# Running the first four attention units of a fused kernel in chunks of 64 tokens, with one decay table instead of two

## The chip, the cores and the metric

The kernel runs on one core of one Trainium2 chip. The metric is device time in microseconds (us) of one execution. Five engines work beside each other, each through its own instructions in order: TensorE (PE; its weight loads are listed as PEld), VectorE (DVE), ScalarE (ACT), GpSimd (POOL) and SyncE (SP), which here only issues DMA transfers. An instruction that needs another engine's result, or a transfer's data, waits on a semaphore, and everything behind it on its engine waits too.

## The reference, cut to what matters

```python
def _attn_ref(q, k, v):                      # (4, 8, 576, 64) each
    scores = np.matmul(q, k.transpose(0, 1, 3, 2)) / np.sqrt(64)
    gamma = 1.0 - 2.0 ** (-5.0 - np.arange(8))
    rel = pos[:, None] - pos[None, :]
    Dmat = np.where(rel >= 0, gamma[:, None, None] ** rel, 0.0)
    return np.matmul(scores * Dmat, v)       # no softmax

x = attn_out.transpose(0, 2, 1, 3).reshape(2304, 512)
h = x @ w_in;  g = h * sigmoid(1.702 * h);  x = g @ w_out        # 512 -> 2048 -> 512
xn = x / sqrt(mean(x * x) + 1e-6) * rms_g
return (silu(xn @ w_gate) * (xn @ w_val)) @ w_out2               # 512 -> 1536 -> 512
```

The attention is linear: a decay per head and distance takes the place of the softmax. So it can be done in pieces of the sequence, with a state S (the decayed sum of k times v over all tokens before) carried from piece to piece. Within a piece the decay gamma^(i-j) is split into a factor for the query (gamma^i / 8, table `qdec`), one for the value (gamma^-j, table `vdec`) and a triangular mask; S is multiplied by a third table, `sdec`, from piece to piece.

## The kernel before

The 2304 tokens are cut into 18 *units* of 128 tokens. The first MLP then takes them in five blocks of 512, 384, 384, 512 and 512 tokens, the second in three of 768. All matmul operands of the MLPs are split in a high and a low part (each product is three matmuls, lines 283 to 285), so x of a unit has to be written as `xh` (rounded, by ACT) and `xl` (the rest, x minus xh).

Block 0 of the first MLP needs x of units 0 to 3, so those four run ahead of it: this is the *front*, written out by hand. The other fourteen units are threaded in between the matmuls of the MLP, in steps given by a table (`at_steps`).

A unit passes through these steps:

- load: q, k and v by DMA from the SP queue (q of unit 0 from ACT's), line 339; packets of 256 bytes
- `a_decay` (line 353): v is multiplied by `vdec` on POOL
- `a_trans` (line 364): eight PE transposes of k and q; ACT copies kT from PSUM (line 371)
- scores, mask, k times v, new state, and out, for which there are two forms

The *wide* form, only for units 0 to 3, takes all 128 tokens as one piece. qT is copied without a factor (lines 375 to 378). Scores are 8 matmuls with 128 columns (line 511), k times v another 8 (line 519), the mask is a multiply by a 128x128 triangle (line 525, DVE), out is 8 matmuls from v and the masked scores (line 569) and 8 from the state and qT (line 555). Only then does the decay of the queries come in, as a multiply on the output (`scaled`, line 583, DVE); ACT makes xh (line 586), POOL or DVE makes xl (line 589). Each unit has an x buffer of its own. Each step of the state is a sum and a multiply by `sdec` (lines 541 and 542).

The *chunk* form, for units 4 to 17, takes two pieces of 64 tokens. qT is multiplied by `qdec` as it leaves PSUM (line 373, DVE). Scores are 16 matmuls with 64 columns (line 396), k times v is 16 (line 405), the mask takes 64 columns per head (line 413), out is 16 matmuls plus 8 for each piece that has a state (line 475). ACT copies the two pieces from PSUM (line 484), DVE adds the two state parts (line 488), ACT makes xh (line 494), POOL xl (line 495). Here all units share one x buffer (`bufs=1`), so the copies of a unit wait until POOL has read x of the unit before.

The two forms want the query decay in different head layouts, so there are two tables in the one tile `qdec`: 256 KB for the front (line 1126, SP queue), and after the last `scaled` of the front a second one, spread over the partitions by two POOL transfers from a row in DRAM (`qrow`, lines 1092 and 1076).

Seven matmuls of a constant (`heat`, line 1103) run on PE before the first data is there. At the end of the front stand the first two weight tiles of the first MLP (`in_halves`: words on ACT, lines 203 and 206; join on DVE, line 209; high part on ACT, line 215; low part on DVE, line 218), and the third by `conv_words` and `conv_join` (lines 189, 190, 243, 252).

Of the kernel before, what the change touches and what calls it, by code (L numbers as in the profile page):

```python
# [21 lines left out]
XB = 512  # L22
# [20 lines left out]
def kernel(  # L43
# [47 lines left out]
    qrow = dram.tile([1, H * 128], F32, name="qrow")  # L91
# [265 lines left out]
    def a_trans(u, where):  # L357
        kr, qr = (raws[u, nm] for nm in "kq")
        pt = a_psum(where)

        more = ps_acc.tile([128, 512], F32, tag="acc", name="at") if u == 0 else pt[0]
        for i, t in ((1, kr), (0, qr)):
            for p in range(HP):
                nc.tensor.transpose(  # L364
                    (more if i == 0 and p > 1 else pt[i])[:, p * 128:(p + 1) * 128],
                    t[:, 2 * p:2 * p + 2, :].rearrange("p h d -> p (h d)"),
                    ident,
                )
        qT = a_tile(u, "qT")
        kT = a_tile(u, "kT")  # L370
        nc.scalar.copy(out=kT, in_=pt[1])
        if u > 3:
            nc.vector.tensor_tensor(out=qT, in0=pt[0], in1=qdec, op=ALU.mult)
        elif u == 0:
            nc.vector.tensor_copy(out=qT[:, :256], in_=pt[0][:, :256])
            nc.scalar.copy(out=qT[:, 256:], in_=more[:, 256:])
# [75 lines left out]
    def a_out(u, where):  # L452
# [30 lines left out]
        for c in range(2):  # L483
            nc.scalar.copy(out=xc[c], in_=po[c][:, :HP * C])
        for c in range(2):
            if old[c]:
                a, b = (t[:, 2 * C * (1 - c):][:, :2 * C] for t in (po[1 - c][:, HP * C:], xc[c]))
                nc.vector.tensor_tensor(out=b, in0=a, in1=b, op=ALU.add)
        x = x.rearrange("p (c a t) -> p a c t", c=2, t=C)
# [3 lines left out]
        def parts():  # L493
            nc.scalar.copy(out=xh, in_=x)  # L494
            nc.gpsimd.tensor_tensor(out=xl, in0=x, in1=xh.bitcast(F32), op=ALU.subtract)  # L495

        rows.append(parts)

    wide_mask = sp.tile([128, TH], F32, tag="norm", name="wide_mask", bufs=3)[:, :2 * C]

    def wide_scores(u, where, amid=lambda: None, own=None):
        qT, kT = st[u]
        sc = a_psum(where)
        for p in range(HP):
            for j in range(2):
                hs = slice(64 * j, 64 * j + 64)  # L510
                nc.tensor.matmul(  # L511
                    sc[j][:, p * 2 * C:(p + 1) * 2 * C], kT[hs, p, :], qT[hs, p, :], start=True, stop=True
                )
        amid()
        kr, vt = raws[u, "k"], raws[u, "v"]
        kv = (own or ps_h.tile([128, XB], F32, tag="h", name="kv"))[:, :HP * D]
        for p in range(HP):
            for j in range(2):
                nc.tensor.matmul(
                    kv[64 * j:64 * j + 64, p * D:(p + 1) * D], kr[:, 2 * p + j, :], vt[:, head(p, j), :],  # L520
                    start=True, stop=True,
                )
        r = [a_tile(u, f"r{j}").rearrange("p (a c) -> p a c", c=2 * C) for j in range(2)]
        for j in range(2):
            nc.vector.tensor_tensor(
                out=r[j], in0=sc[j].rearrange("p (a c) -> p a c", c=2 * C),
                in1=wide_mask.unsqueeze(1).to_broadcast([128, HP, 2 * C]), op=ALU.mult,
            )
        st[u] = (qT, r, kv.rearrange("p (a d) -> p a d", d=D))
        a_free(u, "kT", "k")  # L530

    def wide_state(u, ops=None):
        qT, r, kv = st[u]
        dec = sdec.unsqueeze(2).to_broadcast([128, HP, D])
        old = state["next"] if u else None
        state["next"] = new = att.tile([128, HP, D], F32, tag="S", name="S", bufs=4)
        st[u] = (qT, r, old)

        def sums():
            if old is not None:  # L540
                nc.vector.tensor_tensor(out=new, in0=kv, in1=old, op=ALU.add)
            nc.vector.tensor_tensor(out=new, in0=kv if old is None else new, in1=dec, op=ALU.mult)

        sums() if ops is None else ops.append(sums)

    def wide_at(po, h):
        j, half = h // HP, 64 * x_half(h)
        return po[j][half:half + 64, x_tile(h % HP) * 2 * C:][:, :2 * C]

    def wide_over(po, qT, old, first):  # L550

        for h in (0, 4, 1, 5, 2, 6, 3, 7):
            j, p = divmod(h, HP)
            hs = slice(64 * j, 64 * j + 64)
            nc.tensor.matmul(
                wide_at(po, h), old[hs, p, :], qT[hs, p, :], start=first and x_tile(p) == 0,
                stop=not first and x_tile(p) > 0,
            )

    def wide_out(u, where, po=None):  # L560


        qT, r, old = st.pop(u)
        vt = [raws.pop((u, nm)) for nm in "kqv"][2]
        begun = po is not None
        po = po or a_psum(where)
        for h in range(H):
            j, p = divmod(h, HP)
            nc.tensor.matmul(  # L569
                wide_at(po, h), vt[:, h, :], r[j][:, p, :], start=not begun and x_tile(p) == 0,  # L570
                stop=(begun or old is None) and x_tile(p) > 0,
            )
        if old is not None and not begun:
            wide_over(po, qT, old, False)
        n, o = block_of(2 * C * u)
        a_free(u, "v", "qT", "r0", "r1")
        xh, xl = (t[:, :, o:o + 2 * C] for t in block_tile(n))
        x = a_tile(u, "x")
        xs = x.rearrange("p (k t) -> p k t", t=2 * C)

        def scaled(j):
            js = slice(4 * C * j, 4 * C * j + 4 * C)
            nc.vector.tensor_tensor(out=x[:, js], in0=po[j][:, :4 * C], in1=qdec[:, js], op=ALU.mult)

        def high(ks=slice(0, 4)):
            nc.scalar.copy(out=xh[:, ks], in_=xs[:, ks])  # L586

        def low(ks=slice(0, 4), engine=nc.vector):
            engine.tensor_tensor(out=xl[:, ks], in0=xs[:, ks], in1=xh[:, ks].bitcast(F32), op=ALU.subtract)

        return scaled, high, low
# [422 lines left out]
    with tc.manual_schedule():  # L1014
# [6 lines left out]
        def a_both(u, where):  # L1021

            a_scores(u, where, True)
            a_out(u - 1, HID)
            a_state(u)
# [3 lines left out]
        phases.append((a_out, len(units) - 1))  # L1029
# [35 lines left out]

        a_load(0, "q", nc.scalar)
        a_load(0, "k")
        nc.gpsimd.dma_start(
# [4 lines left out]
        def spread_row(engine, t, row):  # L1073
# [6 lines left out]
        nc.gpsimd.memset(wide_mask, 1.0)  # L1080
        nc.gpsimd.affine_select(
            out=wide_mask, in_=wide_mask, pattern=[[1, 2 * C]], base=0, channel_multiplier=-1,
            compare_op=ALU.is_ge, fill=0.0,
        )
        nc.gpsimd.memset(mask, 1.0)
        for c in range(2):
# [5 lines left out]
        nc.gpsimd.dma_start(  # L1092
            out=qrow.rearrange("o (b e c) -> o b e c", e=2, c=128),
            in_=c_qdec[0:128:64].rearrange("e b c -> b e c").unsqueeze(0),
        )
# [30 lines left out]
        nc.sync.dma_start(out=qdec, in_=c_qdec.rearrange("q b c -> q (b c)"))  # L1126
# [8 lines left out]
        def load_begin(j):  # L1135
# [16 lines left out]

        a_trans(0, AT)
        wide_scores(0, ACC)
        wide_state(0)
        a_trans(1, AT)
        scaled, high, low = wide_out(0, ACC)
        wide_scores(1, ACC)
# [7 lines left out]
        scaled(0)  # L1166
        scaled(1)
        high()
# [8 lines left out]
        scaled, high, low = wide_out(2, ACC)  # L1177
        scaled(0)
        scaled(1)
        high()  # L1180
        join()
        wh()
        word1()
        po = a_psum(AT)
        wide_scores(
            3, ACC, lambda: wide_over(po, st[3][0], state["next"], True),
            ps_acc.tile([128, 512], F32, tag="acc", name="kv"),
        )
        low(engine=nc.gpsimd)
        held_back = []  # L1190
        wide_state(3, held_back)
        scaled, high, low = wide_out(3, ACC, po)
        to_conv.pop(0)
        scaled(0)
        high(slice(0, 2))
        wl()
        join1()
        low(slice(0, 2))
# [292 lines left out]
```

## Time and profile before

| what | before |
|---|---|
| time, median of 3 runs | 884.67 us (884.52 to 885.3) |
| the profiled execution's own time | 885.02 us |
| its span, first to last instruction | 883.3 us |
| PE busy | 876.1 us, 99% of the span |
| DVE, ACT, POOL busy | 512.8, 382.3, 92.0 us |
| first matmul of block 0 | at 24.52 us |
| last idle time of PE ahead of the tail | at 45.23 us, 0.5 us |

The profile is of one execution. Its times count from the first instruction. A timeline row gives start, duration, engine, line, operation, output tile and input tiles, partitions x elements, how many instructions were merged in the row, and in brackets how long the engine stood idle before it and what ended that. A duration of several merged instructions reaches from the first one's start to the last one's end; PE's matmuls overlap, so the distance between two starts tells the pace.

### The profile page before, as it was taken

To read this page: it belongs to the slowest core of one execution; us is meant where nothing else is said; L and a number is where in the kernel's file an instruction comes from. 1 tells how busy PE (TensorE), PEld (TensorE's weight loads), DVE (VectorE), ACT (ScalarE), POOL (GpSimd) and SP (SyncE) were. 2 spreads that over 40 slices of the span, in tenths; PEclk is the share of its full clock that TensorE was granted. 3 is DMA by queue.
4 is the path that set the end of the run, shared out by engine and by line. 5 is a ranking of instruction groups with operands and counts; after the bars stand their busy time and mean duration, and the time that the engine had idled before them with its cause. 6 is when DMAs were issued, how large, how long until landed. Compare 5 with 4: busy or idle time off the path is not lost.

```text
span 883.3 us, 16180 instructions
## 1 busy us (share of the span) xinstructions
PE 876.1 (99%) x6170; PEld 792.8 (90%) x6170; DVE 512.8 (58%) x918; ACT 382.3 (43%) x766; POOL 92.0 (10%) x100
## 2 busy tenths in 40 slices
PE   9999999999999999999999999999999999999998
PEld 7778889999999888888889999999999999999997
DVE  4778754464574555756645557765575666333444
ACT  3877754365445554564463343334322225112222
POOL 4201111131232212311200000000000000000000
PEclk9999999999999999999999999999999999999999
DMA  9986445689789987897777766557654556555552
GB/s 217 265 282 193 131 156 168 205 318 313 234 256 317 280 258 243 268 398 255 258 273 228 242 213 213 167 167 252 224 153 158 155 155 227 160 163 158 164 168 107
DMA packets 153200, 193.49 MB, mean 219 GB/s; under 512 B 66144, under 2 KB 94052, under 8 KB 153124
## 3 DMA queue, kind: packets, MB, share of 16 engines
q1 hardware_dynamic: 144212, 165.06, 60.0%
q10 hardware_dynamic: 8688, 27.14, 9.3%
q8 instruction: 49, 0.80, 0.4%
q0 software_dynamic: 224, 0.27, 0.1%
q14 instruction: 27, 0.22, 0.1%
HBM read 150.22 MB, written 42.21 MB: 218 GB/s over the span
## 4 chain that ended last, share of the span: by engine, by line
PE 96%; ACT 1%; DVE 1%; DMA 0%; issue 0%; SPq 0%; DVEq 0%; ACTq 0%
PE h L283 17%; PE h L285 17%; PE h L284 17%; PE acc L283 11%; PE acc L285 11%; PE acc L284 11%; PE v L284 2%; PE v L285 2%; PE v L283 2%; PE at L364 2%; PE at L475 1%; PE at L396 1%; PE at L405 1%; PE at L511 1%; DMA wslots<-in_k_dram 0%; PE at L569 0%
## 5 line engine op out<-in xcount | busy, mean ns | idle before, releaser
L283 PE MATMUL h<-fast 128*128 128x384 f32 (+1 forms) x824 | 288.4, 350 | 1.1 <-ACT fast L586 0.6
L285 PE MATMUL h<-fast 128*128 128x384 f32 (+1 forms) x824 | 287.1, 348 | 0.0
L284 PE MATMUL h<-fast 128*128 128x384 f32 (+1 forms) x824 | 286.6, 348 | 0.1
L917 DVE TENSOR_TENSOR wslots<-h,wslots 128x384 f32<-128x384 f32 x180 | 100.2, 556 | 151.6 <-PE h L285 151.2
L283 PE MATMUL acc<-fast 128*128 128x512 f32 (+1 forms) x464 | 174.9, 377 | 0.0
L285 PE MATMUL acc<-fast 128*128 128x512 f32 (+1 forms) x464 | 174.5, 376 | 0.0
L284 PE MATMUL acc<-fast 128*128 128x512 f32 (+1 forms) x464 | 174.3, 376 | 0.0
L283 PEld LDWEIGHTS h<-fast 128*128 128x128 f32 x824 | 154.7, 188 | 10.9 <-ACT fast L586 0.8
L284 PEld LDWEIGHTS h<-fast 128*128 128x128 f32 x824 | 154.8, 188 | 9.3 <-DVE fast L218 0.5
L285 PEld LDWEIGHTS h<-fast 128*128 128x128 f32 x824 | 154.6, 188 | 8.2 <-DVE fast L255 0.4
L609 DVE TENSOR_TENSOR fast<-g,fast 128x512 fp32r<-128x512 f32 (+1 forms) x80 | 53.9, 673 | 123.8 <-ACT fast L607 123.1
L950 ACT CAST fast<-g 128x384 fp32r<-128x384 f32 x36 | 18.5, 514 | 219.6 <-DVE g L920 219.6
L627 ACT ACTIVATE g<-h 128x512 f32<-128x512 f32 (+1 forms) x80 | 44.3, 553 | 136.4 <-PE h L285 136.4
L285 PEld LDWEIGHTS acc<-fast 128*128 128x128 f32 x464 | 87.1, 188 | 13.3
L283 PEld LDWEIGHTS acc<-fast 128*128 128x128 f32 x464 | 87.1, 188 | 12.7
L284 PEld LDWEIGHTS acc<-fast 128*128 128x128 f32 x464 | 87.1, 188 | 11.9
L868 DVE TENSOR_TENSOR wslots<-wslots 128x256 fp32r<-128x256 f32 x84 | 43.6, 555 | 14.8 <-ACT wslots L867 14.8
L840 POOL TENSOR_TENSOR wslots<-wslots 128x256 f32<-128x256 f32 x48 | 43.2, 919 | 76.0 <-DVE wslots L243 63.1
L607 ACT CAST fast<-g 128x512 fp32r<-128x512 f32 (+1 forms) x80 | 46.2, 578 | 2.5
L495 POOL TENSOR_TENSOR fast<-x,fast 128x512 fp32r<-128x512 f32 x14 | 18.7, 1339 | 227.5 <-ACT fast L494 203.8
L189 ACT ACTIVATE sslots<-sslots 128x512 f32<-128x512 f32 x56 | 37.7, 674 | 0.2 <-DMA sslots<-in_moe_w_out_dram 0.2
L190 ACT ACTIVATE sslots<-sslots 128x512 uint32<-128x512 uint8 x56 | 37.0, 661 | 0.0
(137 smaller groups left out, 872.2 us busy)
## 6 DMA issues: line engine op xcount, KB each, us to landing
fast<-up_d SPq DMA_DIRECT2D x252, 256.0 KB, 3.0
fast<-out_d ACTq DMA_DIRECT2D x51, 512.0 KB, 5.1
up_d<-wslots SPq DMA_DIRECT2D x84, 256.0 KB, 4.9
sslots<-in_moe_w_out_dram SPq DMA_DIRECT2D x19, 512.0 KB, 5.2
out_d<-fast SPq DMA_DIRECT2D x16, 512.0 KB, 3.6
sslots<-in_moe_w_in_dram SPq DMA_DIRECT2D x15, 512.0 KB, 4.9
sslots<-in_moe_w_val_dram SPq DMA_DIRECT2D x12, 512.0 KB, 6.4
sslots<-in_moe_w_gate_dram SPq DMA_DIRECT2D x11, 512.0 KB, 6.1
```

Of the source, the lines that this page charges most:

```text
L189: nc.scalar.activation(out=hi, in_=hi, func=AF.Prelu, scale=2.0 ** -112, alpha=-(2.0 ** 32))
L190: nc.scalar.activation(out=lo, in_=byte, func=AF.Copy, scale=1 / 32, bias=-31 / 64)
L283: nc.tensor.matmul(ps, lh, rh, start=first, stop=False, skip_group_check=more)
L284: nc.tensor.matmul(ps, *pairs[0], start=False, stop=False, skip_group_check=more)
L285: nc.tensor.matmul(ps, *pairs[1], start=False, stop=last, skip_group_check=more)
L495: nc.gpsimd.tensor_tensor(out=xl, in0=x, in1=xh.bitcast(F32), op=ALU.subtract)
L607: nc.scalar.copy(out=gh, in_=g)
L609: nc.vector.tensor_tensor(out=gl, in0=g, in1=gh.bitcast(F32), op=ALU.subtract)
L627: nc.scalar.activation(out=g, in_=ps, func=AF.Gelu_apprx_sigmoid)
L840: nc.gpsimd.tensor_tensor(out=o, in0=a, in1=b, op=op)
L868: nc.vector.tensor_tensor(out=wl.bitcast(F32R), in0=w, in1=wh, op=ALU.subtract)
L917: nc.vector.tensor_tensor(out=o, in0=a, in1=b, op=ALU.add)
```

## The change

Units 0 to 3 take the chunk form too. The whole wide form goes (`wide_scores`, `wide_state`, `wide_over`, `wide_out`, the 128x128 mask, the x buffer per unit). `a_out` hands back its four last steps (copies, adds, high, low), so that the front can order them by hand; `a_rows` keeps the old order for the later units.

The two tables give way to one in the layout of the chunk form. Columns 0 to 64 of it are loaded at the very start, in four transfers of 64 partitions x 2 x 65 numbers (`decay_load`: two from POOL ahead of everything there, two from SP behind k of unit 0); columns 65 to 127 are made by one DVE instruction as a product of two loaded ones.

```diff
+        nc.vector.tensor_tensor(out=qT, in0=pt[0], in1=qdec, op=ALU.mult)
         if u > 3:
-            nc.vector.tensor_tensor(out=qT, in0=pt[0], in1=qdec, op=ALU.mult)
-        elif u == 0:
...
-        else:
-            nc.scalar.copy(out=qT, in_=pt[0])
-        a_decay(u)
+            a_decay(u)
...
-        for c in range(2):
-            nc.scalar.copy(out=xc[c], in_=po[c][:, :HP * C])
...
+        def copies():
+            for c in range(2):
+                nc.scalar.copy(out=xc[c], in_=po[c][:, :HP * C])
...
+        return copies, adds, high, low
...
+        def decay_load(e, queue):
+            for j in range(2):
+                queue.dma_start(
+                    out=qdec[64 * j:64 * j + 64].rearrange("p (b e c) -> p b e c", b=2, e=2)[:, :, e, :C + 1],
+                    in_=c_qdec[64 * e:64 * e + 64, 2 * j:2 * j + 2, :C + 1],
+                )
+
+        decay_load(0, nc.gpsimd)
         a_load(0, "q", nc.scalar)
         a_load(0, "k")
+        decay_load(1, nc.sync)
...
-        nc.gpsimd.dma_start(
-            out=qrow.rearrange("o (b e c) -> o b e c", e=2, c=128),
...
-        nc.sync.dma_start(out=qdec, in_=c_qdec.rearrange("q b c -> q (b c)"))
...
+        q_c = qdec.rearrange("p (a c) -> p a c", c=2 * C)
+        nc.vector.scalar_tensor_tensor(
+            out=q_c[:, :, C + 1:], in0=q_c[:, :, 1:C], scalar=float(D) ** 0.5,
+            in1=q_c[:, :, C:C + 1].to_broadcast([128, HP, C - 1]), op0=ALU.mult, op1=ALU.mult,
+        )
+
+        def begin_scores(u):
+            a_scores(u, ACC, True)
+            a_state(u, (0,))
+
+        def begin_out(u):
+            copies, adds, high, low = a_out(u, HID)
+            copies()
+            adds()
+            high()
+            return low
...
-        low(engine=nc.gpsimd)
-        wide_state(1)
-        scaled, high, low = wide_out(1, ACC)
-        scaled(0)
-        scaled(1)
-        high()
-        wide_scores(2, ACC)
-        low(engine=nc.gpsimd)
-        wide_state(2)
+        a_state(1, (1,))
+        a_decay(2)
+        low = begin_out(1)
+        low()
+        begin_scores(2)
         a_trans(3, AT)
+        a_state(2, (1,))
+        a_decay(3)
         (word, join, wh, wl), (word1, join1, wh1, wl1) = in_halves(0)
         word()
...
+        low = begin_out(2)
+        low()
         join()
         wh()
+        begin_scores(3)
         word1()
...
+        copies, adds, high, low = a_out(3, HID)
+        copies()
+        join1()
+        adds()
+        wh1()
+        high(slice(0, 2))
+        wl()
+        low(slice(0, 2), nc.vector)
...
-        spread_row(nc.gpsimd, qdec, qrow)
```

How the instructions stand on the engines shows where work moved. First PE, from the scores of unit 3 to the first matmul of block 0. Before, in the wide form (line 511 scores, 555 state part of out, 519 k times v, 569 value part of out):

```order
L511 MATMUL at<-wslots 128x128 [waits Activation_49]
L511 MATMUL at<-wslots 128x128 [waits PE_49]
L511 MATMUL at<-wslots 128x128 x6
L555 MATMUL at<-wslots,S 64x128 [waits DVE_49,PE_49]
L555 MATMUL at<-wslots,S 64x128 [waits PE_49]
L555 MATMUL at<-wslots,S 64x128 x6
L519 MATMUL kv<-wslots 64x64 [waits DVE_49,Pool_49]
L519 MATMUL kv<-wslots 64x64 x7
L569 MATMUL at<-wslots 64x128 [waits DVE_49]
L569 MATMUL at<-wslots 64x128 x3
L569 MATMUL at<-wslots 64x128 [waits DVE_49]
L569 MATMUL at<-wslots 64x128 x3
```

The same place in the changed kernel (line 389 scores, 398 k times v, 468 out):

```order
L389 MATMUL at<-wslots 64x64 [waits DVE_49,Activation_49]
L389 MATMUL at<-wslots 64x64 x15
L398 MATMUL at<-wslots 64x64 [waits Pool_49]
L398 MATMUL at<-wslots 64x64 x15
L468 MATMUL at<-wslots 64x64 [waits DVE_49,Activation_49]
L468 MATMUL at<-wslots 64x64 x7
L468 MATMUL at<-wslots 64x64 [waits DVE_49]
L468 MATMUL at<-wslots 64x64 x7
L468 MATMUL at<-wslots,S 64x64 x8
L468 MATMUL at<-wslots,S 64x64 [waits DVE_49]
L468 MATMUL at<-wslots,S 64x64 x7
L282 MATMUL h<-fast 128x512 [waits Activation_49]
```

The state part of out, which stood ahead of k times v and of POOL's decayed v, now stands behind both, at the end of the unit.

Second ACT, from the first words of the weights to the last of x (before: line 586 makes xh; 203 and 206 words, 215 high part of weights):

```order
L203 ACTIVATE sslots<-sslots 128x256 [waits DMAHW5_49]
L206 ACTIVATE sslots<-sslots 128x256
L586 CAST fast<-wslots 128x4x128 [waits DVE_49]
L215 CAST fast<-ww 128x256 [waits DVE_49]
L203 ACTIVATE sslots<-sslots 128x256 [waits DMAHW7_49]
L206 ACTIVATE sslots<-sslots 128x256
L586 CAST fast<-wslots 128x2x128 [waits DVE_49,Activation_49]
```

In the changed kernel (line 482 copies x from PSUM, 491 makes xh; 202, 205 and 214 are the weights' lines):

```order
L202 ACTIVATE sslots<-sslots 128x256 [waits DMAHW6_49]
L205 ACTIVATE sslots<-sslots 128x256
L482 COPY x<-at 128x256 [waits PE_49,Pool_49]
L482 COPY x<-at 128x256 [waits PE_49]
L491 CAST fast<-x 128x4x128 [waits DVE_49,Activation_49]
L214 CAST fast<-ww 128x256 [waits DVE_49]
L202 ACTIVATE sslots<-sslots 128x256 [waits DMAHW0_49]
L205 ACTIVATE sslots<-sslots 128x256
L482 COPY x<-at 128x256 [waits PE_49,Pool_49]
L482 COPY x<-at 128x256 [waits PE_49]
L214 CAST fast<-ww 128x256 [waits DVE_49]
L491 CAST fast<-x 128x2x128 [waits DVE_49,Activation_49]
```

Two copies per unit came in on ACT, and the first of them waits for POOL, which reads the shared x buffer.

Third DVE, from the start to the first multiply of x of unit 0. Before:

```order
L375 COPY wslots<-at 128x256
L525 TENSOR_TENSOR wslots<-at,wide_mask 128x512 x2
L542 TENSOR_TENSOR S<-kv,sdec 128x256
L525 TENSOR_TENSOR wslots<-at,wide_mask 128x512 x2
L583 TENSOR_TENSOR wslots<-at,qdec 128x256 x2
```

In the changed kernel (line 1064 makes the rest of the table, 370 is qT, 406 the mask, 431 to 440 the state, 488 the adds):

```order
L1064 SCALAR_TENSOR_TENSOR qdec<-qdec 128x4x63
L370 TENSOR_TENSOR wslots<-at,qdec 128x512
L406 TENSOR_TENSOR wslots<-at,mask 128x4x64 x2
L431 COPY S<-at 128x256
L370 TENSOR_TENSOR wslots<-at,qdec 128x512
L439 TENSOR_TENSOR S<-at,S 128x256
L440 TENSOR_TENSOR S<-S,sdec 128x256
L488 TENSOR_TENSOR x<-at,x 128x128
```

The table `qdec`, first read by the multiply of the first output, is now read ahead of the first scores.

## Rows read from the trace of the kernel before

**Rows 1.** Busy time by stretch: start:end, length, engines' busy us, PEclk, DMA, GB/s.

```profile
8.60:24.50 15.90, 15.31 (x256) 12.64 (x252) 10.86 (x23) 7.19 (x16) 7.03 (x6) 1.00 1.14 262
```

**Rows 2.** PE's waits over the whole run: us in total, times, longest.

```profile
PE h L283 <- DVE fast L252: 0.5, 1, 0.5
```

**Rows 3.** Chain of waits from 24 to 46 us: start, us, what.

```profile
24.82 0.32 ACT sslots L206
...
27.04 0.74 ACT fast L215 x2
27.79 0.58 ACT sslots L189
...
28.96 0.70 DVE ww L243
29.69 0.62 ACT fast L252
...
44.66 0.44 DVE fast L252
...
45.23 0.47 PE h L283
```

**Rows 4.** Timeline, all engines, unit 3 at the end of the front.

```profile
18.48 0.42 PEld L364 LDWEIGHTS at<-ident,wslots 128*128 128x128 f32 x4 [0.24 <-PE at L364]
...
20.23 1.04 POOL L353 TENSOR_TENSOR wslots<-wslots,vdec 128x512 f32<-128x512 f32 x1 [1.12 <-DMA wslots<-in_v_dram]
...
22.36 1.28 POOL L589 TENSOR_TENSOR fast<-wslots,fast 128x512 fp32r<-128x512 f32 x1 [1.09 <-ACT fast L586]
...
24.07 0.40 ACT L586 CAST fast<-wslots 128x256 fp32r<-128x256 f32 x1 [0.84 <-DVE wslots L583]
...
24.52 0.50 PE L283 MATMUL h<-fast 128*128 128x512 f32 x1 [0.58 <-ACT fast L586]
```

**Rows 5.** Timeline, a later unit in chunk form; the first row is another unit's qT.

```profile
46.94 0.69 DVE L373 TENSOR_TENSOR wslots<-at,qdec 128x512 f32<-128x512 f32 x1
...
56.52 0.69 PE L396 MATMUL at<-wslots 64*64 64x64 f32 x32
57.03 0.65 PE L405 MATMUL at<-wslots 64*64 64x64 f32 x32
57.50 0.65 PE L475 MATMUL at<-wslots 64*64 64x64 f32 x32
57.80 0.76 DVE L413 TENSOR_TENSOR wslots<-at,mask 128x256 f32<-128x256 f32 x2 [1.92 <-PE at L405]
57.97 0.41 PE L475 MATMUL at<-wslots,S 64*64 64x64 f32 x16
...
58.43 0.65 ACT L484 COPY x<-at 128x256 f32<-128x256 f32 x2 [3.27 <-PE at L475]
...
59.11 0.29 DVE L488 TENSOR_TENSOR x<-at,x 128x128 f32<-128x128 f32 x1 [0.55 <-ACT x L484]
...
59.77 0.42 DVE L446 TENSOR_TENSOR S<-at,S 128x256 f32<-128x256 f32 x1
```

**Rows 6.** Timeline, all engines, units 0 and 1.

```profile
1.43 0.73 POOL L1068 DMA_DIRECT2D srow<-in_sdec_dram  x1 [0.92 <-POOLq L1473]
...
5.90 1.08 POOL L1076 DMA_DIRECT2D sdec<-srow  x2 [1.42 <-DMA srow<-in_sdec_dram]
...
7.23 1.94 PE L511 MATMUL at<-wslots 64*128 64x128 f32 x16 [0.18 <-DVE wslots L375]
...
11.76 1.16 PE L511 MATMUL at<-wslots 64*128 64x128 f32 x16
```

**Rows 7.** DMA view, 0 to 24.5 us in 40 slices; issues: KB each, us to landing.

```profile
GB/s 0 0 0 86 248 281 240 201 220 215 217 219 217 218 211 206 212 217 223 269 299 265 220 240 209 225 259 189 224 209 202 255 278 323 358 344 363 393 364 258
...
qdec<-in_qdec_dram SPq DMA_DIRECT2D x1, 256.0 KB, 4.0
...
srow<-in_sdec_dram POOLq DMA_DIRECT2D x1, 0.0 KB, 4.2
```

More of the change, by code (lines that the diff above doesn't have):

```diff
@@ L359, in a_trans @@
         pt = a_psum(where)
-        more = ps_acc.tile([128, 512], F32, tag="acc", name="at") if u == 0 else pt[0]
         for i, t in ((1, kr), (0, qr)):
@@ L364, in a_trans @@
                 nc.tensor.transpose(
-                    (more if i == 0 and p > 1 else pt[i])[:, p * 128:(p + 1) * 128],
+                    pt[i][:, p * 128:(p + 1) * 128],
                     t[:, 2 * p:2 * p + 2, :].rearrange("p h d -> p (h d)"),
@@ L482, in a_out @@
         xc = [x[:, HP * C * c:HP * C * (c + 1)] for c in range(2)]
-        for c in range(2):
-            nc.scalar.copy(out=xc[c], in_=po[c][:, :HP * C])
[L485 to L489, printed above, removed]
+        xs = x.rearrange("p (c a t) -> p a c t", c=2, t=C)
@@ L490, in a_out @@
         xh, xl = (t[:, :, o:o + 128].rearrange("p a (c t) -> p a c t", t=C) for t in (xh, xl))
         a_free(u, "v", "qT", "r0", "r1")
[L493 to L585, printed above, removed]
@@ L586, in high, with adds, low @@
+        def copies():
+            for c in range(2):
+                nc.scalar.copy(out=xc[c], in_=po[c][:, :HP * C])
+        def adds():
+            for c in range(2):
+                if old[c]:
+                    a, b = (t[:, 2 * C * (1 - c):][:, :2 * C] for t in (po[1 - c][:, HP * C:], xc[c]))
+                    nc.vector.tensor_tensor(out=b, in0=a, in1=b, op=ALU.add)
+        def high(ks=slice(0, KD)):
             nc.scalar.copy(out=xh[:, ks], in_=xs[:, ks])
-        def low(ks=slice(0, 4), engine=nc.vector):
+        def low(ks=slice(0, KD), engine=nc.gpsimd):
@@ L589, in low, with a_rows @@
             engine.tensor_tensor(out=xl[:, ks], in0=xs[:, ks], in1=xh[:, ks].bitcast(F32), op=ALU.subtract)
-        return scaled, high, low
+        return copies, adds, high, low
+    def a_rows(u, where):
+        copies, adds, high, low = a_out(u, where)
+        copies()
+        adds()
+        rows.append(lambda: (high(), low()))
     G = {}
@@ L1028 @@
         phases += [(fn, u) for u in range(5, len(units)) for fn in (a_trans, a_both)]
-        phases.append((a_out, len(units) - 1))
+        phases.append((a_rows, len(units) - 1))
         at_steps = (
@@ L1079 @@
         make_identity(nc, ident)
[L1080 to L1084, printed above, removed]
         nc.gpsimd.memset(mask, 1.0)
@@ L1180 @@
-        high()
+        low = begin_out(2)
+        low()
         join()
         wh()
+        begin_scores(3)
         word1()
[L1184 to L1194, printed above, removed]
+        last_front = st[3]
@@ L1195 @@
+        copies, adds, high, low = a_out(3, HID)
+        copies()
+        join1()
+        adds()
+        wh1()
         high(slice(0, 2))
         wl()
-        join1()
-        low(slice(0, 2))
+        low(slice(0, 2), nc.vector)
+        to_conv.pop(0)
         (next_word, join, wh, next_wl), (word2, join2, wh2, wl2) = in_halves(1)
+        to_conv.pop(0)
+        high(slice(2, 4))
+        low(slice(2, 4), nc.vector)
         next_word()
-        wh1()
-        to_conv.pop(0)
-        scaled(1)
@@ L1204 @@
-        spread_row(nc.gpsimd, qdec, qrow)
-        high(slice(2, 4))
-        low(slice(2, 4))
-        for u in range(4):
-            a_free(u, "x")
         wl1()
@@ L1216 @@
         wl2()
-        held_back.pop()()
+        st[3] = last_front
+        a_state(3, (1,))
+        del st[3]
         conv_words(*to_conv[0])
```

23 lines of the change are left out of this document (7 added, 16 removed).

## The prediction

> **What bounds the kernel now.** I read four views. The busy time by stretch says that PE is busy for 15.31 of the 15.9 us from 8.6 to 24.5 [rows 1], so the front looks bound by PE, and the change takes PE work out of it. That reading is too quick: what matters is what the last unit waited for. In the timeline POOL stood still for 1.12 us until v of unit 3 had landed, at 20.23; and PE's second half of the transposes of unit 3 (q) began at 18.48 after a small pause that ends where q of unit 3 lands (the row names PE; I take the transfer, because this half is the one that needs it) [rows 4]. The DMA rate stands at 200 to 290 GB/s from 2.5 us until then [rows 7], without a hole: the front is fed as fast as packets of 256 bytes arrive. So PE's matmuls fill time that would else be spent waiting for q and v. Block 0 starts at 24.52, 4.3 us after v of unit 3 [rows 4].
>
> Next, what the start of block 0 is worth. PE waits only once more ahead of the tail: 0.5 us for DVE [rows 2], at 45.23. The chain of waits shows why: from the last x of the front it runs over ACT and DVE (first and third weight tile, line 243 at 28.96, line 252 at 29.69) and comes back to PE only at 45.23 [rows 3]. So between 24.5 and 45.2 the path is ACT's and DVE's, and PE may start up to 0.5 us later for nothing. What counts is when line 252 of the third weight tile comes: 29.69. After 45.23 PE is never late again, so what is lost or won at 45 stays to the end.
>
> **PE's work.** A unit in the chunk form costs, by the distance between starts, 0.51 for scores, 0.47 for k times v, 0.47 for the value part of out and 0.41 at most for each piece's state part [rows 5], 2.3 us in all beside the transposes. Transposes are twice 0.42 [rows 4], so some 3.1 us a unit. In the wide form PE is busy for 15.31 us between 8.6 and 24.5 [rows 1], in which it does unit 0 from k times v on and units 1 to 3, some 3.6 units: 4.25 each. So about 1.1 us a unit are saved; the scores alone, 1.16 against 0.69 [rows 5, 6], give 0.5 as a lower end. Over four units 2 to 5 us. All of it lies beside the waiting for q and v, so I count it as nothing, except as slack against the items below; if the data came earlier it would be worth what they came earlier, not more.
>
> **The table, and the first unit.** The first scores now wait for qT, that for `qdec`, that for four transfers and one DVE instruction. Two go out from POOL, ahead of `srow`, which took 4.2 us from issue to landing [rows 7] and 0.73 to issue at 1.43 [rows 6]. So the second leaves at about 2.2 and lands at 6.4; SP's two, behind k, land within that. DVE makes the rest in some 0.4 (nearest is the mask, 128x256 twice in 0.76 [rows 5]): 6.9, just ahead of the last transposes (7.1). Then qT, 0.69 [rows 5], and PE's scores at 8.0 instead of 7.23 [rows 6]. `srow` now leaves 1.3 us later and `sdec` with it (5.90 to 7.2), and POOL decays v of unit 0 only behind that, 8.3 to 9.3; k times v at 9.5. That is 0.4 us late against before, but unit 3's q at 18.4 takes it up: by my list of all steps the transposes of unit 3 have 1.1 us of room. Cost 0. No gain lies here, since nothing of unit 0 gets earlier; at the other end, loads that took 8.4 us, twice `srow`'s, would bring the table at 11, and the front would be late by 1.7.
>
> **The queue.** 256 KB of table leave SP's queue ahead of v of unit 2. At 215 to 290 GB/s [rows 7] that is 0.9 to 1.2 us of service. The four new pieces are 133 KB, 0.6 us at 215. So units 1 and q, k of unit 2 come 0.6 later (room as above), v of unit 2 and all of unit 3 between 0 and 0.6 earlier, and 1.2 at most if the new pieces fit wholly in the empty first 2 us. SP issues one DMA more in all; I take 0, since it is the DMA engines that are full, not SP. The 256 KB that went from `qrow` at 25.6 on are gone too; weights land a little earlier, and none of the waits in [rows 2] is for them: 0.
>
> **From unit 3's data to block 0.** Two chains now meet in the copies of x of unit 3.
> Values: v decayed at 20.23 + 1.04 = 21.27 [rows 4], k times v on PE 21.4 to 21.9, out with both state parts 1.0 (0.47 [rows 5], and for two state parts 0.5; 0.8 at most). But out also needs the masked scores, and DVE is now busy with qT, two state steps (some 0.4 each, like half of the mask), the adds of unit 2 and a join, so the mask (0.76) ends at 22.3; out runs from 22.5 to 23.5.
> The x buffer: q at 18.4, transposes to 18.9, qT to 19.6, out of unit 2 to 19.9; ACT has kT and two operations on the first weight words (0.32 each [rows 3]) until 20.0, copies (0.65 [rows 5]) to 20.7, adds on DVE (twice 0.29 [rows 5]) to 21.25, xh (0.40 for a half [rows 4], 0.62 for all) to 21.9, POOL's xl 1.28 [rows 4] to 23.3. Only then may unit 3's copies begin: 23.4.
> So copies 23.5 to 24.15 (ACT, 0.65), adds to 24.75, xh of the first half to 25.15 (0.40 [rows 4]), PE at 25.3. Before, one multiply and one cast stood there. **Block 0 starts 0.8 us later** (0.2 to 1.4).
>
> **To line 252.** With x done early for both halves, ACT goes on: xh of the second half to 25.5, four weight operations at 0.33 [rows 3] to 26.85, two casts (0.74) with their joins to 27.7, line 189 and 190 at 0.57 each [rows 3] to 28.85, the join 0.70 to 29.55, so the counterpart of line 252 at 29.6, against 29.69. Before, ACT idled in this stretch for DVE, which still had a `scaled` to do; now it does not. So the ACT and DVE chain is not later (-0.1, from -0.7 to +0.6), and PE, 0.8 late, uses up the 0.5 of room at 45.23 [rows 2] and 0.3 more. The later of the two counts: **+0.3 us**, between -0.6 (everything at its early end) and +0.9.
>
> The profiled execution took 885.02 us (span 883.3 and 1.7 around it), so the sum is 885.3 for it; it was 0.35 above the median of the runs, 884.67. Forecast for the median: 885.0. About 0.2%, 1.8 us, is what a measurement of this kernel can tell from no change, so the forecast is "no change".
>
> **Rivals.**
> *PE's saving shows.* For it: PE is 96% busy from 8.6 to 24.5 [rows 1]. Against it: v of unit 3. Its landing plus decay, out, copies, adds and cast, with no queue anywhere, is 24.7. Only earlier data help: at the best 1.2 us, block 0 at 24.1 and line 252 some 0.9 earlier: 883.8, still within 0.2%. To be faster by more, SP's queue would have to run ahead by 2 us.
>
> [...]
>
> *The table is late.* Four small transfers, two from POOL, now stand ahead of everything. Price: one for one beyond 1.1 us of room; at the upper end above 1.7, that is 886.7. For it: DMA is full from 2.5 us. Against: 33 KB pieces early in the queue.
>
> **Chances.** Forecast 0.62, data earlier 0.16, clock 0.13, table late 0.09. The likeliest case by itself spans 884.1 to 885.6. Faster by over 0.2% has only the far end of the second case and what I overlook: 0.06. Slower by over 0.2% (above 886.4): three quarters of the clock, half of the late table, and a little of the forecast: 0.17. Same: 0.77. The range takes in the earlier data (883.8) and the middle of the clock and table cases: 883.7 to 887.0.
>
> **What would show it.** In the new profile: POOL's decay of unit 3 at 20 to 20.5, still behind v; first matmul of block 0 at 25.3; copies of x of unit 3 behind POOL's xl of unit 2 or behind PE, within 0.2 us of each other; line 251 (the old 252) at 29.6; PE's wait at 45 gone, or nearly, instead of 0.5; PE busy down by 2 to 6 us before 25. Wrong if v of unit 3 lands ahead of 19.2, if block 0 starts ahead of 24.2 or behind 26, or if its first matmuls stand twice as far apart as later ones.

## The result: 0.84% slower, and the profile after

The changed kernel takes **891.76 us** (median; 891.52 to 894.0), against 884.67 for the kernel before in the same session; the ratio is 1.0084 (95% interval 1.0069 to 1.0098). The forecast of 885.0 (883.7 to 887.0) was wrong. The profiled execution took 891.52 us, its span is 889.8, 6.5 more than before.

The waits of PE over the whole run (us in total, times, longest) already show that the time went before block 0. Nothing later than 31 us is in this list; the wait at 45 us [rows 2] is gone.

```profile
PE at L398 <- issue: 3.6, 1, 3.6
PE at L389 <- DVE wslots L370: 2.1, 1, 2.1
PE h L282 <- ACT fast L491: 1.9, 1, 1.9
...
PE at L362 <- issue: 1.1, 1, 1.1
...
PE at L468 <- DVE wslots L406: 0.6, 1, 0.6
```

Two of them are of a kind that the profile before did not have: "issue", that is, PE stood still and waited for no engine and no transfer that the profile knows. Here is PE's timeline from the scores of unit 0, and of its end from unit 3's transposes on:

```profile
8.46 1.14 PE L389 MATMUL at<-wslots 64*64 64x64 f32 x32 [2.09 <-DVE wslots L370]
...
18.59 0.66 PE L362 MATMUL at<-ident,wslots 128*128 128x128 f32 x4
20.34 0.63 PE L362 MATMUL at<-ident,wslots 128*128 128x128 f32 x4 [1.10 <-issue]
20.90 0.69 PE L468 MATMUL at<-wslots 64*64 64x64 f32 x32
21.42 0.65 PE L468 MATMUL at<-wslots,S 64*64 64x64 f32 x32
21.88 0.66 PE L389 MATMUL at<-wslots 64*64 64x64 f32 x32
22.35 0.63 PE L398 MATMUL at<-wslots 64*64 64x64 f32 x26
26.55 0.34 PE L398 MATMUL at<-wslots 64*64 64x64 f32 x6 [3.57 <-issue]
27.49 0.70 PE L468 MATMUL at<-wslots 64*64 64x64 f32 x32 [0.60 <-DVE wslots L406]
...
30.85 0.79 PE L282 MATMUL h<-fast 128*128 128x512 f32 x1 [1.87 <-ACT fast L491]
```

The second stop falls into the middle of a group, after 26 matmuls of 32, where nothing new is needed: only the first of them has a wait in the list of PE's order above. The first stop falls between the transposes of unit 3's k and those of its q, so its place alone doesn't tell. But by the landing times in the trace the last piece of that q was there at 18.16 us, and PE stopped at 19.24. Between the two stops stand 4 + 32 + 32 + 32 + 26 = **126 matmuls**; each has a weight load beside it (6426 of either in the whole run), so that is 252 records. Unit 3's v was there long before (POOL decays it at 20.85, against 20.23 in [rows 4]); ACT's copies of x of unit 3 come at 29.06 and wait for PE alone:

```profile
20.85 1.04 POOL L352 TENSOR_TENSOR wslots<-wslots,vdec 128x512 f32<-128x512 f32 x1 [0.19 <-DMA wslots<-in_v_dram]
...
29.06 0.65 ACT L482 COPY x<-at 128x256 f32<-128x256 f32 x2 [3.99 <-PE at L468]
...
35.26 0.62 ACT L251 CAST fast<-ww 128x512 fp32r<-128x512 f32 x1 [0.76 <-DVE ww L242]
```

Block 0 starts at 30.85 instead of 24.52 [rows 4], the counterpart of line 252 comes at 35.26 instead of 29.69 [rows 3]. The last three columns of the view by stretch (granted clock, DMA share, GB/s) show the third thing, PE's clock:

```profile
10.00:15.00 5.00, 5.00 (x140) 4.55 (x132) 2.82 (x7) 1.31 (x4) 1.04 (x1) 0.55 1.25 203
15.00:25.00 10.00, 6.72 (x278) 5.76 (x268) 6.72 (x17) 5.77 (x14) 5.41 (x5) 1.00 0.98 278
25.00:30.00 5.00, 1.83 (x70) 1.53 (x69) 1.60 (x5) 1.01 (x4) 0.47 (x1) 0.81 0.53 87
30.00:35.00 5.00, 4.15 (x10) 3.28 (x11) 4.60 (x13) 4.04 (x11) 0.00 (x0) 0.50 0.80 246
```

It fell from 1.00 to 0.50 twice: at 7.7 us, within the 2.09 us in which PE waited for the table, back at 1.00 from 14.5; and at 28.1, ahead of block 0 and 1.6 us after the stop of 3.57, until 35.0. Before, it stood at 1.00 from 8.6 us on [rows 1].

### The profile page after: what moved, and what is told of

It is laid out like the page before. It is cut to its first block, busy times and chain, and to the rows that moved or that the text cites. A ratio compares the mean times of both kernels' runs of the same rounds, so it can differ in the third digit from the quotient of the medians.

```text
span 889.8 us, 16697 instructions
## 1 busy us (share of the span) xinstructions
PE 874.7 (98%) x6426; PEld 793.0 (89%) x6426; DVE 515.8 (58%) x926; ACT 383.3 (43%) x770; POOL 91.4 (10%) x97
## 4 chain that ended last, share of the span: by engine, by line
PE 97%; issue 1%; DMA 0%; DVE 0%; ACT 0%; POOL 0%; SPq 0%; DVEq 0%; ACTq 0%
PE h L282 17%; PE h L284 17%; PE h L283 17%; PE acc L282 11%; PE acc L284 11%; PE acc L283 11%; PE at L468 2%; PE v L283 2%; PE v L284 2%; PE v L282 2%; PE at L362 2%; PE at L389 1%; PE at L398 1%; DMA qdec<-in_qdec_dram 0%; ACT x L482 0%
## 5 line engine op out<-in xcount | busy, mean ns | idle before, releaser
L494 POOL TENSOR_TENSOR fast<-x,fast 128x512 fp32r<-128x512 f32 x17 | 22.6, 1331 | 238.9 <-ACT fast L491 198.2
```

## The experiments

Three theories. **A**: PE runs out of instructions. They come to it by DMA, and the chunk form uses them faster than they come. The queue table of the page has a line for it (packets, MB, share of the engines), first before, then changed:

```profile
q8 instruction: 49, 0.80, 0.4%
```

```profile
q8 instruction: 51, 0.84, 0.4%
```

That is 16 KB a packet, and two packets more for 512 records more on PE (256 matmuls and their weight loads), so some 256 instructions a packet.

**B**: some data comes late because of the new transfers. **C**: the clock alone. In the kernels derived from the changed one, line numbers shift by a few.

### Taking instructions away, adding them, moving them

**The changed kernel with its front's matmuls merged in pairs of heads**: half the instructions, the same columns.

```diff
-        for p in range(HP):                     # scores; k times v and out likewise
+        for p in range(0, HP, w):               # w = 2 for units 0 to 3
-   sc[j][cs, p * C:(p + 1) * C], kT[hs, p, cs], qT[hs, p, cs]
+   sc[j][cs, p * C:(p + w) * C], kT[hs, p, cs], qT[hs, p:p + w, cs]
```

> The changed kernel, with the matmuls of units 0 to 3 (scores, k times v, both parts of out) merged in pairs of heads: one matmul of 128 columns where two of 64 stood, so the second head of a pair gets the first one's operand and the output isn't the reference's. 163 matmuls ahead of block 0 instead of 287; same columns, same transfers, same work on the other engines. Theory A: the 1.1 and 3.6 us of idle time that the profile puts down to issue are gone, block 0 starts at 25 to 27 instead of 30.85, the time is 885.5 to 888. Theory B: block 0 still at 29.5 or later and the time above 890. Theory C: PE is as idle as before or more, the clock still falls ahead of block 0, time at 889 or above.

886.94 us, ratio 1.0012 (1.0003 to 1.0022): of the loss of 7.1 us 1.1 is left, each against the kernel before in its own session (884.67 and 885.83), so 6.0 us are gone. No "issue" wait is left, and block 0 is at 26.26. PE's timeline shows why this is a clean comparison: a group takes the same time with half the matmuls (x16 in 0.67, in the changed kernel x32 in 0.69).

```profile
20.06 0.62 PE L473 MATMUL at<-wslots,S 64*64 64x128 f32 x16
20.51 0.67 PE L390 MATMUL at<-wslots 64*64 64x128 f32 x16
21.74 0.67 PE L400 MATMUL at<-wslots 64*64 64x128 f32 x16 [0.56 <-POOL wslots L352]
...
26.26 0.50 PE L282 MATMUL h<-fast 128*128 128x512 f32 x1 [1.95 <-ACT fast L496]
```

**Five constant matmuls between the transposes and the scores of unit 0**, in the changed kernel:

```diff
         a_trans(0, AT)
+        warm_up(5)
```

> The changed kernel with five more constant matmuls between the transposes and the scores of unit 0, where PE stood idle for 2.1 us (20 PE instructions more ahead of everything behind). Theory A: the two stalls stay and stand 20 instructions earlier in the work: the k times v of unit 3 breaks off after some 16 of its 32 records instead of 26. Time 890 to 893. Theory C: the clock does not fall at 7.7 any more, the first two units run at full speed; if the clock were the cause, block 0 would start 2 us or more earlier and the time be 889 or less.

893.35 us, 1.0087 (1.0070 to 1.0104), 0.35 us above A's range. The clock is now at 1.00 from the first scores until 25.9 us, within the second stop, and still nothing is gained. The stops moved earlier in the work, and the count between them stayed: 6 + 8 + 32 + 32 + 32 + 16 = 126.

```profile
16.97 0.67 PE L398 MATMUL at<-wslots 64*64 64x64 f32 x26
19.25 0.34 PE L398 MATMUL at<-wslots 64*64 64x64 f32 x6 [1.61 <-issue]
...
21.99 0.42 PE L398 MATMUL at<-wslots 64*64 64x64 f32 x16
27.94 0.71 PE L398 MATMUL at<-wslots 64*64 64x64 f32 x16 [5.52 <-issue]
```

From the start of the program, constant matmuls included, both kernels have 346 matmuls ahead of the first stop: a place in the program's stream, not in the work. That speaks against B and C.

**The kernel before with its wide matmuls halved**, 88 matmuls more in the code:

```diff
-   wide_at(po, h), vt[:, h, :], r[j][:, p, :]          # scores and state part likewise
+   wide_at(po, h)[:, cs], vt[:, h, :], r[j][:, p, cs]  # for c in range(2), 64 columns each
```

> The kernel before, with every score and out matmul of the front cut in two halves of 64 columns (88 matmuls more, 247 instead of 159 ahead of block 0, four PE instructions each); same data, same transfers, same waits, same result. Theory A (PE runs out of instructions: it gets them in blocks of 256 and a new block needs 5 to 6 us while the DMA queues are full): PE shows idle time put down to issue, of 0.5 to 3 us, in the middle of a group, 256 instructions apart (at about its 705th and perhaps its 961st instruction); block 0 starts 1 to 4 us later than 24.5, and the time is 886 to 889. Theory B (the data come late because of the new transfers): nothing here is changed in the data, so no idle time of that kind and block 0 within 0.8 us of 24.5 (the matmuls themselves get a little longer), time 884.5 to 885.5. Theory C (the clock falls because PE idles): as B.

888.35 us, 1.0036 (1.0023 to 1.0049): in the expected range, but not for the expected reason. PE has no "issue" wait over 0.4 us, where A expected 0.5 to 3. Block 0 came at 27.41, 2.9 us later, because a scores group takes 2.05 us instead of 1.16 [rows 6]:

```profile
17.11 2.05 PE L512 MATMUL at<-wslots 64*128 64x64 f32 x32
```

Three such groups are 2.7 us of work, nearly all of the loss. A unit's 120 matmuls last 5.4 us there (17.11 to the next scores at 22.54), with the DMA engines moving 281 GB/s (15 to 25 us), and PE did not stop. So more matmuls alone made no stop; the changed kernel used up its 126 in 2.64 us. The 5 to 6 us that A allowed for a block was an estimate; what the changed kernel shows is 6.2 us from one restart of PE to the next.

**The mechanism by itself**: the kernel before, with 128 constant matmuls of 64x64 behind unit 3's transposes, and, as its companion, with 16 of 128x128 instead.

```diff
         a_trans(3, AT)
+        for i in range(128):     # quadrants in turn, as in the chunk form
+            nc.tensor.matmul(more[j][cs, ...64], one[hs, :64], one[hs, 64:], start=True, stop=True)
```

> The kernel before, unchanged but for 128 matmuls of a constant (64x64, 64 columns each, in the pace of the chunk form: 32 in 0.51 us) on PE between the transposes of unit 3 and the out part of unit 2: 256 more instructions (with the weight loads) and some 2.0 us more of PE work, and nothing that waits for data. A: PE stands still once, with nothing to wait for ('issue'), 1 to 3 us, between the small matmuls and the end of the front; block 0 at 27.6 to 29.7 (24.52 before), 888.2 to 890.3 us. Without A: only the 2.0 us of work, no such wait: block 0 at 26.5, 887 us, as its companion with 16 large matmuls.

> The companion: the kernel before with 16 matmuls of a constant (128x128, 128 columns, 0.13 us each by the pace of the transposes) at the same place, so the same 2.1 us of PE work in 32 instructions instead of 256. All theories: no 'issue' wait above 0.3 us; the front of the kernel before has PE busy from 7.2 to 23.9 without a gap, so block 0 comes 2.0 later, at 26.5, and the time is 886.5 to 887.3 us. If that front were fed by the transfers, as the prediction had it: less than 1 us later, 885 to 886 us.

The companion took 888.43 us, 1.0033 (1.0022 to 1.0045), the small ones 896.37 us, 1.0125 (1.0101 to 1.0148). In the traces, first the companion and then the small ones:

```profile
19.29 3.74 PE L1178 MATMUL heat<-ones 128*128 128x128 f32 x32
22.96 1.09 PE L569 MATMUL at<-wslots 128*64 128x128 f32 x16
...
28.41 0.50 PE L283 MATMUL h<-fast 128*128 128x512 f32 x1 [0.58 <-ACT fast L586]
```

```profile
18.92 2.55 PE L1180 MATMUL heat<-ones 64*64 64x64 f32 x156
25.62 2.73 PE L1180 MATMUL heat<-ones 64*64 64x64 f32 x100 [4.15 <-issue]
```

I had both amounts of work wrong by two, and both times lie above the ranges expected: a matmul of this type in the code stands as two in the trace (x32 for 16, x256 for 128). The work is not quite equal, 3.7 us against 5.2, as the last 100 small ones run largely at the lower clock (granted 0.58 from 25.62 to 28.28, 1.00 for the first 156). The comparison still holds: only the many small ones stop, for 4.15 us, among constants that wait for nothing, after again 346 matmuls. These 4.15 are most of the 5.95 us between the two starts of block 0 (34.36 and 28.41). This shows A at a place where no attention work stands. The companion shows a second thing: 3.67 us of work made block 0 3.9 us later, so PE was the bound of the front before.

### Where the refill waits

**All four table loads from POOL** (B's test):

> The changed kernel with all four table loads issued by POOL, none by SP, so that SP issues k of unit 1 in its old place (at 2.4 instead of 4.3). Theory B: the data of units 1 to 3 land earlier by 1 us or more, block 0 at 29.8 or earlier, time 890.5 or less. Theory A: the start of block 0 hangs on the blocks of instructions, so less than 0.7 us either way; the table itself comes later, as POOL issues two more.

895.55 us, 1.0103 (1.0088 to 1.0119). The first scores wait 3.83 us for the table and start at 10.24; block 0 comes at 33.69, 2.8 later than in the changed kernel, and both stops are there (1.91 and 3.30 us). By the landing times unit 3's q is there at 18.2 us as in the changed kernel and its v at 20.1 instead of 20.8, so the run moved the data less than B supposed. It shows no gain for B, but doesn't price data that come a full microsecond earlier.

**The weights held back**, so that the DMA engines are free ahead of the second stop:

```diff
         a_state(2, (1,))
+        nc.sync.dma_start(out=scrap[:1, 15:16], in_=state["next"][:1, 0, :1])   # SP waits here
+        load() ...                              # moved here from ahead of the front
```

> The changed kernel, with all loads from the second weight tile on and those of unit 4 held on SP until the state after unit 2 is there (about 22.5 us in the changed kernel); no other instruction changes. A, with the refill of instructions waiting behind data in the DMA engines: the first stall (1.1 us at 20.3) stays, as the loads ahead of it are the same; the second (3.6 us at 26.5) shrinks to under 1 us; block 0 at 27 to 28.5, 888 to 889.5 us, if the held weights do not come late. A with a fixed time of refill: the second stall stays at 3 to 4 us, 891.5 us or more. B or C: the waits stay as they are and the weights come late, 892 us or more.

890.33 us, 1.0055 (1.0039 to 1.0071). The second stop shrank from 3.57 to 0.57 us; the first stayed (1.33), as expected. Block 0 came at 27.69, 3.2 earlier. The time stays 0.8 us above what I expected: in the two traces the span is only 1.5 shorter (888.3 against 889.8), though the two ratios are 0.29% apart, which is 2.6 us. Some of what the trace lost went in block 0's first twelve products, which take 5.3 us instead of 4.8, as the clock is low until 33.4 (0.43 us from one product to the next until then, 0.23 after); where the rest went is not shown. In this kernel's trace:

```profile
22.45 0.68 PE L398 MATMUL at<-wslots 64*64 64x64 f32 x26
23.69 0.34 PE L398 MATMUL at<-wslots 64*64 64x64 f32 x6 [0.57 <-issue]
```

The DMA view between the two stops (40 slices of the window, share busy in tenths, then packets by queue), first of the changed kernel, 20.34 to 26.55, then of this one, 20.16 to 23.69:

```profile
DMA  9999988999999899999999999999999999999887
...
q8 instruction: 1, 0.02, 1.1%
```

```profile
DMA  0000010000000800000000000000000000000000
...
q8 instruction: 1, 0.02, 1.8%
```

In each, one instruction packet comes within the window, and PE goes on after it. By the packets' own times in the trace it runs from 23.90 to 25.02 in the changed kernel and from 21.39 to 22.43 here, and PE goes on 1.5 and 1.3 us after its end. So what the data traffic adds stands ahead of the packet: it starts 3.6 us after PE last went on in the one, 1.2 in the other. From one restart of PE to the next it took 6.2 us with busy DMA engines and 3.5 with idle ones. In the changed kernel PE took 2.64 us for its 126 matmuls (20.34 to 22.98). No run here shows less than 3.5.

### What is left without the stops: the clock and the data

**Merged and filled**: the merged kernel with the five constant matmuls.

> The changed kernel with the front's matmuls merged in pairs of heads (second head of each pair gets the first's operand, so this part of the computation is another one), and five constant matmuls ahead of the scores of unit 0, so that PE does not idle while the table is made. The merged kernel without them took 886.94 us, block 0 at 26.25, and PE at the lower clock from 7.88 to 14.71. Instruction supply (A): no idle time 'issue' above 0.3 us; block 0 at 25.3 to 26.0, since v of unit 3 (20.6) then sets the end; 885.9 to 886.9 us. Clock as the main loss (C): the 2.5 us that the matmuls lost between 7.9 and 14.7 all come back: block 0 at 23.8, 884.5 us. Late data (B): no change against the merged kernel, 886.9 us.

886.48 us, 1.0013 (1.0003 to 1.0022). Block 0 at 25.45, inside A's range, and the time too. In the profiled run, the fastest of the ten, the clock stood at 1.00 throughout (the others list 0.996 to 1.000). v of unit 3 sets the end:

```profile
19.79 1.30 POOL L352 TENSOR_TENSOR wslots<-wslots,vdec 128x512 f32<-128x512 f32 x1 [1.04 <-DMA wslots<-in_v_dram]
...
21.14 0.67 PE L400 MATMUL at<-wslots 64*64 64x128 f32 x16 [0.93 <-POOL wslots L352]
...
21.86 0.76 DVE L408 TENSOR_TENSOR wslots<-at,mask 128x256 f32<-128x256 f32 x2 [0.48 <-PE at L400]
...
22.43 0.69 PE L473 MATMUL at<-wslots 64*64 64x128 f32 x16 [0.62 <-DVE wslots L408]
...
23.66 0.65 ACT L487 COPY x<-at 128x256 f32<-128x256 f32 x2 [0.93 <-PE at L473]
...
25.45 0.50 PE L282 MATMUL h<-fast 128*128 128x512 f32 x1 [1.89 <-ACT fast L496]
...
29.81 0.62 ACT L251 CAST fast<-ww 128x512 fp32r<-128x512 f32 x1 [0.76 <-DVE ww L242]
```

**The same with an x buffer for each unit**, and **the changed kernel with that alone**:

```diff
-        x = att.tile([128, 512], F32, tag="x", name="x", bufs=1)
+        x = a_tile(u, "x") if u < 4 else att.tile([128, 512], F32, tag="x", name="x", bufs=1)
```

> The merged kernel with the five constant matmuls (second head of each pair gets the first's operand), and each of units 0 to 3 with an x buffer of its own, as the kernel before had it. If the shared x buffer sets the end of the front once instructions come in time (copies of x of unit 3 behind POOL's xl of unit 2, as in the prediction): 0.5 to 1 us less than the same kernel with the shared buffer. If v of unit 3 sets it: within 0.3 us of that kernel.

> The changed kernel with an x buffer of its own for each of units 0 to 3. A: the copies of x of unit 3 wait for PE (29.06 us), not for POOL (xl of unit 2 done at 25.46), so nothing changes: 891.3 to 892.3 us, block 0 at 30.8, both stalls as before. If the shared buffer is what makes the front late: 889 to 890.5 us.

886.14 us, 1.0011 (1.0001 to 1.0020): 0.34 us less, between the two expectations. But block 0 is at 25.56, no earlier than with the shared buffer (25.45), and in both traces the copies of x of unit 3 wait for PE, not for POOL. So v sets the end and not the shared buffer. In the changed kernel alone it took 893.83 us, 1.0095 (1.0077 to 1.0113), above the range expected, with block 0 at 32.34 and stops of 1.8 and 2.4 us. Neither run shows a gain from the buffer that is clear of noise. The second lies 2 us above the changed kernel, 0.1% by the two ratios, whose intervals overlap. In its trace the first stop is longer (1.8 us instead of 1.1), and the clock is low from 21.6 to 25.0 us as well; why the stop is longer was not settled.

**The changed kernel repaired as far as it goes** (weights held, constant matmuls, own x buffers), and the same with 12 more constant matmuls behind unit 3's out part:

> The changed kernel with three repairs: weights held as in the earlier run, five constant matmuls ahead of the first scores, own x buffers for units 0 to 3. A: the front starts 2 us earlier by the clock, but the stalls for instructions stay in part (0.5 to 2 us each); block 0 at 26 to 27.7, first matmuls of block 0 at the lower clock again (PE idle before them); 888 to 890 us. If instructions were no limit: block 0 at 25.4 as in the merged kernel, 886.5 us.

> As the run with three repairs, and 12 constant matmuls on PE behind the out part of unit 3, in the 1.9 us in which PE waits for the first x of block 0. A plus clock: block 0 starts at the same time within 0.3 us, its first twelve matmuls take 3.3 us instead of 4.8 to 5.3, and the time is 1 to 2 us less than in that run (887 to 888.5). If the clock does not depend on this: no difference.

889.40 us, 1.0044 (1.0028 to 1.0060), and 889.67 us, 1.0045 (1.0029 to 1.0062). The stops remain (1.6 and 1.1 us in the first). The second keeps the clock at 1.00 from 25 to 35 us, where the first has 0.54 and then 0.77. Its twelve first products took 2.9 us instead of 4.9, so the clock is worth 2.0 us there; but its fill, twice as long as meant, pushed block 0 from 27.85 to 28.64, and the time lies above the 887 to 888.5 expected. The first product behind the second transposes in block 0 came 20.3 us after the block's start instead of 21.5: of the 2.0 us 1.2 is left, as PE waits 0.66 us at 41.99 for POOL's decayed v of a later unit. Nothing was gained in sum, and neither run reaches the kernel before.

## Why the prediction was wrong, point by point

**The step that failed is PE's work.** It was priced by busy time alone: shorter groups, "so I count it as nothing". It looked for what shorter groups would save at least, and not for what more instructions could cost. The same time on PE holds many more instructions now: PE has 6426 matmuls instead of 6170, all 256 of them ahead of block 0, and the stretch from 20.34 to 22.98 uses up 126 of them with their weight loads. That takes 2.6 us, and from one restart of PE to the next it was 3.5 (DMA engines idle, the run with the weights held) to 6.2 (busy). So a term put at nothing cost two stops, 1.1 and 3.6 us, and made block 0 4.6 us late.

**Where 6.3 us of block 0 went.** The changed kernel's block 0 at 30.85 became 26.26 without stops, 25.45 with the clock held as well, and is 24.52 in the kernel before: 4.6 us are the supply, 0.8 the clock in the front, 0.9 the chain from v of unit 3. These shares are read from the merged kernels. In block 0 the first twelve products take 4.76 us instead of 3.35, at the lower clock (0.50 until 35.0), so the distance grows to 7.7 (35.61 against 27.87). By the first product behind the second transposes the changed kernel needs 21.37 us (30.85 to 52.22), the kernel before 20.71 (24.52 to 45.23, with the wait of 0.5, which the changed kernel no longer has): 7.0 apart. Eight products on it is 6.8 (54.13 against 47.36) and stays so until 480 us; the last products are 6.6 apart, the spans 6.5. What gives the last 0.3 us is not shown.

**The bound of the front was misread.** "The front is fed as fast as packets of 256 bytes arrive" took the first reading, PE busy for 15.31 of 15.9 us [rows 1], for too quick. That first reading was right: 3.67 us of added constants made block 0 3.9 later. POOL's wait for v [rows 4] was real, but PE had other work meanwhile. How much less PE work would bring before v sets the end was not measured in the wide form.

**The chain from v of unit 3 was right in the main.** It shows only once the stops and the low clock are out of the way. In the merged and filled kernel v is decayed at 19.79 (forecast 20 to 20.5), block 0 starts at 25.45 (forecast 25.3), line 251 comes at 29.81 (forecast 29.6). One detail missed in it: unit 3's mask waits for k times v (DVE goes on behind line 400 there, line 398 in the changed kernel); scores and k times v stand in the same PSUM tile. The forecast of +0.3 us comes near that kernel's span (883.8 against 883.3), but partly by luck: PE, 0.9 late at block 0, does not use up the wait at 45 us there; it waits 0.77 us at 45.98, longer than before. And that run is the fastest of ten; the ratio of 1.0013 has 1.0003 as its lower end.

**The x buffer** was named as one of two chains that end within 0.2 us of each other. In the merged kernel without constants they do: PE is done with unit 3's out at 24.31, and the copies wait for POOL a little longer.

```profile
24.47 0.65 ACT L487 COPY x<-at 128x256 f32<-128x256 f32 x2 [0.40 <-POOL fast L499]
```

With constants the buffer is free earlier and v sets the end; in the changed kernel PE's stops do. **The table** came 0.5 us later than forecast (first scores at 8.46, not 8.0). By itself that costs nothing, as forecast: in the filled merged kernel they start at 8.42, and v sets the end. Indirectly it costs clock: in the changed kernel that falls to 0.50 at 7.7, within the wait for the table, and with five constant matmuls in the gap it stays at 1.00 until 25.9. **The clock** was given 0.13, and the range takes in the middle of that case with its upper end, 887.0. No run shows that figure for the clock alone, and in the front of the kernel before the clock stands at 1.00 from 8.6 to 24.5 us [rows 1]. The last of the marks named came: the first products stand 0.43 us apart, later ones 0.23. What the runs show of its price is 0.8 us in the front of the merged kernel; in block 0 the first twelve products take 1.4 us longer than before and 2.0 longer than at the higher clock, of which 0.7 to 1.2 is left behind the second transposes. It explains the smaller part of the loss. **The wait at 45.23** is gone in the changed kernel, but since block 0 is 6.3 us late there, not for the reason forecast.

## What to carry to other kernels

Before you cut matmuls into smaller ones, count PE's instructions in the densest stretch and not only their time. Here PE stopped where 126 matmuls with their weight loads lasted 2.6 us, and did not where 120 lasted 5.4; where between the two it begins was not measured. No wait in the profile of before announces it. The mark is an "issue" wait in the middle of a group of like matmuls, at a place that stays fixed in the stream when the work is moved. To learn which engine bounds a stretch, add a known amount of idle work to it and see how much of it arrives at the end.

## What the runs showed of the hardware that was not expected

- The refill of PE's instructions: one packet of 16 KB per 256 (51 packets instead of 49 for 512 records more). From one restart of PE to the next 3.5 us with idle DMA engines (the run with the weights held), 4.3 in the two repaired kernels (busy in the first microsecond only), 6.2 with busy ones (the changed kernel), and up to 8.7 (19.25 to 27.94, in the kernel with five constant matmuls). The changed kernel and the one with five constant matmuls stop after 346 matmuls and again after 126 more, the kernel with the 128 small constants after 346.
- Two kernels with nearly equal busy time on PE (874.7 and 873.0 us) and equal transfers differ by 6.0 us, each against the kernel before in its session, through the number of matmuls alone (x16 in 0.67 us against x32 in 0.69).
- A matmul with 64 rows of weights by 128, on 64 columns, was hardly cheaper than on 128: 32 took 2.05 us in the kernel with halved wide matmuls (the scores), 16 wide ones 1.16 in the kernel before. With 128 rows by 64 it was: 32 took 1.20 us there (the value part of out), 16 wide ones 1.09.
